# A gated mix of a spectral filter and a product-key lookup on one core: x tiles repeated by ScalarE, narrow inverse pieces joined, gates moved, another level of minima, a new order

## The chip, the cores and the metric

One NeuronCore of a Trainium2 chip runs the whole kernel in one launch. The metric is device time in microseconds, the median of several executions. Engines are named as the profile names them: PE (TensorE, matmuls), DVE (VectorE), ACT (ScalarE), POOL (GpSimd, here only the issuer of gathers) and SP (the issuer of plain loads and stores).

## The reference, cut to what matters

```
# x: (2048, 576); H = 32 heads, E = 64, dk = 128; u, v: (4096, 576)
g = sigmoid((x * gate_w).sum(-1, keepdims=True))
a = irfft2(rfft2(x) * (w_r + 1j * w_i))           # over the 2048 rows and the 576 columns
q = einsum("nd,dhc->nhc", x, w_q)                 # c = 2 * dk
s1, s2 = q[..., :dk] @ k1.T, q[..., dk:] @ k2.T   # (2048, 32, 64) each
i1, i2 = argmax(s1), argmax(s2)                   # top-1 of each; t1, t2 the scores there
e = i1 * 64 + i2                                  # one row of u and v for each token and head
p = softmax(one score)                            # 1, since one candidate is left
b = sum over h of  p * gelu(x . u[e]) * v[e]
out = g * a + (1 - g) * b
```

All of it is fp32. Each token needs 32 rows of u and v, gathered by an index that the scores give.

## The kernel before, in words

The 2048 tokens are 16 tiles of 128. The 32 heads are 8 chunks of 4. Tiles 0 to 9 are early (`E_T`), tiles 10 to 15 late (`L_SEQ`).

**Scores.** For each chunk `build_m` multiplies the keys into w_q (a high and a low part), and `scores` makes the scores of two tiles in a PSUM bank pair with 28 matmuls of 128x512. DVE takes the maxima (L385), ACT the signs of score minus maximum (L392), and then the position of the maximum is found in bf16: two halvings by `min` (L405, L413), a ramp added (L414), and a reduce over the 16 that are left (L416). The indices go to `ei` (early tiles) and `eil` (late ones).

**Early gathers.** `group(t, c)` issues four indirect DMAs on POOL (L465), one for each head of the chunk; each brings 128 rows of u and v (1152 numbers a partition) into a `uv` buffer. DVE multiplies with x and sums (the dot, L472, two instructions in the trace: the main one and the read of the accumulator), ACT applies gelu, and the v rows are added into `xn` in one of three ways, which the table `ROWS` picks: bit k set means that ACT scales the row (L493) and DVE adds it (L494), a clear bit a multiply-add on DVE (L498), and the value 16 sends the group through PE with a diagonal matrix (`dg`, L508).

**Late gathers.** For tiles 10 to 15 the 128 partitions are four heads by 32 tokens, so that one gather covers four heads. `quad(t, c)` issues four of them (L549), DVE makes the dots (L554) and PE sums over the heads with 16 narrow passes. For the dots each block of 32 tokens of x must stand on all four partition groups: `repeat(t)` does that on PE, with a matrix of identities (`rp`), for four blocks in two halves of the columns, and ACT drains each half out of PSUM (L541).

**Gates.** `gates(t, w)` is a DVE multiply with a sum over the columns, of x and the gate weights. The weights are spread over the partitions by `spread`: a load of one row, a matmul with a row of ones, a drain. This happens twice: for the early tiles near the start (L331), for the late ones in `close_gates` (L333), which then makes the sigmoid and its scalings `gsc` and `gone`.

**The transform.** `fold`, `f2`, `f4`, `f5` and `f6` are its steps in and back; `unit_back` does the first inverse step for a pair of frequencies: two pieces, each with eight passes of 256 columns into one bank (main) and four narrow passes into the other (the last 33 or 32 columns), drained by ACT (L806, L809). `invert` does the second inverse step; its result is scaled by `gsc` on ACT, and `mix` adds the lookup's part times `gone`.

**What sets the order.** Every operation is a job in a plan; the table `ORDER`, a list of job numbers, fixes in which order they are issued, and each engine runs its jobs in that order. Buffers come from rings: `uv` has 12 slots and gets more as other tiles die: the pairs that hold eight early x tiles (`pair0` to `pair3`), the area of the sign work and the room of the scores' operands. PSUM is four bank pairs (`bank`). Score pieces, repeats, transform pieces and sums share them.

Of the kernel before, what the change touches and what calls it, by code (L numbers as in the profile page):

```python
# [154 lines left out]
def tile_kernel(ctx, tc, xn, xT, x5, wqT, wq5, kT, wri, uv, gw, t_kr, t_fi, t_tw, t_io, out):  # L155
# [135 lines left out]
    lq = pp.tile([P, NL, H], F32, tag='lq', name='lq')  # L291
# [70 lines left out]
    def scores(c, tp):  # L362
# [53 lines left out]
        dv(0.06 + n * 256 / 960, lambda: nc.vector.tensor_reduce(im.ap[:, :2 * n].rearrange('p a h b -> p (a h b)'), q2()[:, :, :Q], AX.X, ALU.min), [im], keys)  # L416
# [110 lines left out]
    def repeat(t, after):  # L527
        x = xs[t]
        xr[t] = [buf(('xr', 'xn'), [P, D]) for _ in range(HPC)]
        for h in (0, 2):  # L530
            for r in range(2):
                ps = psum()
                cols = slice(r * 288, r * 288 + 288)

                def go(h=h, cols=cols, ps=ps):
                    for n in range(2):
                        lo = QB * (h + n)
                        mm(ps.ap[:, n, :288], rp.ap[lo:lo + QB, :], x.ap[lo:lo + QB, cols], start=True, stop=True)
                plan('PE', 0.7, go, [ps], [rp, x], after=after)
                for n in range(2):  # L540
                    ac(act(288), lambda n=n, h=h, cols=cols, ps=ps: actv(xr[t][h + n].ap[:, cols], ps.ap[:, n, :288], AF.Copy), [(xr[t][h + n], r)], [ps])  # L541
# [595 lines left out]
```

## Time and profile before

| what | us |
|---|---|
| median of three runs (lowest, highest) | 931.17 (930.18, 937.04) |
| the profiled execution | 935.08 |
| its span, first to last instruction | 933.3 |
| PE, DVE, ACT, POOL busy in the span | 870.9, 823.3, 594.9, 574.3 |
| share of the DMA queues: gathers, loads and stores | 84.9%, 11.6% |
| first gather issued | 34.41 |
| first quad's dot | 600.0 |

How to read it: a busy engine is one that has an instruction in flight, and durations of neighbours overlap, so a group's busy time can be less than its count times the mean of one; what an instruction costs a full engine is read from start to start. The shares are means over stages with different limits, so the prediction takes the busy times by stage, and the chain of waits (followed back from the last instruction) by stage. The DMA share is the time in which packets were under way, and GB/s what they moved. An fp32 matmul is two passes, two instructions in the trace.

### The profile page before, as it was taken

Reading aid. Unit: us, or ns where it says so; the run is one execution under the profiler, and the core shown is the slowest. Engines: PE = TensorE matmul, PEld = TensorE weight load, DVE = VectorE, ACT = ScalarE, POOL = GpSimd, SP = SyncE. Lnnn points to the kernel's source line nnn. Section 1 sums busy time; section 2 is a strip of 40 time slices with the busy share of each in tenths; the row PEclk is TensorE's granted clock in tenths of the full one; section 3 lists DMA queues with packets and bytes.
Section 4 is the critical chain, followed back from the end, with each engine's and each line's share of the span. In section 5 each row is a group of like instructions: output and inputs, shape, how many; then the busy total and the mean of one; then the engine's idle time right before and its main releaser. Section 6 shows DMA issues by size and latency. Waiting matters only on the chain.

```text
span 933.3 us, 16536 instructions
## 1 busy us (share of the span) xinstructions
PE 870.9 (93%) x5306; PEld 657.7 (70%) x5306; DVE 823.3 (88%) x1999; ACT 594.9 (64%) x2097; POOL 574.3 (62%) x516
## 2 busy tenths in 40 slices
PE   7999999999999999999999986788999989799986
PEld 6887888778877878787877775566565656466554
DVE  4899999999999999999999989999796867857577
ACT  5797988788868887979977869643333213232222
POOL 0366566765666766575667766677575666657561
PEclk9999999999999999999999998789999989999898
DMA  9999999999999999999999999999999998989997
GB/s 303 340 332 395 359 351 370 345 384 382 340 366 387 372 386 376 364 368 369 356 385 402 353 387 413 372 365 398 389 350 377 383 419 311 385 317 390 392 342 301
DMA packets 89467, 342.41 MB, mean 367 GB/s; under 512 B 9954, under 2 KB 10594, under 8 KB 89380
## 3 DMA queue, kind: packets, MB, share of 16 engines
q0 software_dynamic: 73728, 302.02, 84.9%
q1 hardware_dynamic: 15652, 39.33, 11.6%
q8 instruction: 42, 0.69, 0.3%
q14 instruction: 45, 0.37, 0.1%
HBM read 336.59 MB, written 4.72 MB: 366 GB/s over the span
## 4 chain that ended last, share of the span: by engine, by line
PE 49%; DVE 26%; ACT 8%; DMA 8%; issue 5%; another core or an unknown queue 2%; POOL 1%; DVEq 0%; SPq 0%; ACTq 0%
PE bank L256 49%; DVE uv L472 7%; DMA uv<-uv,ei 5%; DVE uv L554 4%; DVE xn L498 3%; DVE xn L494 3%; ACT area L392 3%; DVE area L385 2%; DMA pair<-uv,eiq 2%; DMA uv<-uv,eiq 1%; DVE pair L554 1%; ACT area L400 1%; DVE area L405 1%; DVE xn L522 1%
## 5 line engine op out<-in xcount | busy, mean ns | idle before, releaser
L465 POOL DMA_INDIRECT uv<-uv,ei x316 | 359.9, 1139 | 228.9 <-issue 61.8
L256 PE MATMUL bank<-mh,xt 128*128 128x512 f32 x768 | 261.6, 397 | 0.2 <-issue 0.2
L392 ACT ACTIVATE area<-bank,area 128x64 bf16<-128x64 f32 x1024 | 221.8, 352 | 20.8 <-DVE area L385 13.6
L549 POOL DMA_INDIRECT uv<-uv,eiq x141 | 155.0, 1099 | 88.8 <-PE bank L256 47.1
L472 DVE SCALAR_TENSOR_TENSOR uv<-uv,pair 128x576 f32<-128x576 f32 x253 | 184.9, 750 | 6.8 <-DMA uv<-uv,ei 5.5
L256 PE MATMUL bank<-ml,xt 128*128 128x512 f32 x448 | 174.8, 390 | 0.0
L256 PEld LDWEIGHTS bank<-mh,xt 128*128 128x128 f32 x768 | 144.2, 188 | 31.3 <-issue 0.7
L256 PE MATMUL bank<-uv,dg 128*32 128x288 f32 (+2 forms) x888 | 146.5, 416 | 13.7 <-ACT dg L508 5.5
L256 PE MATMUL bank<-mhx,xt 128*128 128x512 f32 x384 | 136.4, 402 | 0.2 <-DVE xn L522 0.2
L256 PEld LDWEIGHTS bank<-uv,dg 128*32 128x32 f32 (+2 forms) x888 | 82.6, 140 | 54.0 <-issue 9.7
L256 PE MATMUL bank<-fi,bt 128*128 128x289 f32 x384 | 106.1, 430 | 5.4 <-DVE area L750 2.4
L554 DVE SCALAR_TENSOR_TENSOR uv<-uv,xr 128x576 f32<-128x576 f32 x141 | 103.3, 752 | 6.5 <-DMA uv<-uv,eiq 2.9
L256 PEld LDWEIGHTS bank<-fi,bt 128*128 128x128 f32 x384 | 85.2, 247 | 27.3 <-issue 6.8
L498 DVE SCALAR_TENSOR_TENSOR xn<-uv,a,xn 128x576 f32<-128x576 f32 x125 | 101.2, 811 | 0.1
L256 PEld LDWEIGHTS bank<-ml,xt 128*128 128x128 f32 x448 | 84.2, 188 | 16.5
L493 ACT ACTIVATE uv<-uv,a 128x576 f32<-128x576 f32 x101 | 76.2, 777 | 13.9 <-DVE a L483 8.8
L256 PEld LDWEIGHTS bank<-mhx,xt 128*128 128x128 f32 x384 | 72.3, 188 | 17.9 <-ACT area L392 1.3
L385 DVE TENSOR_REDUCE area<-bank 128x16 f32<-128x1024 f32 x64 | 77.7, 1216 | 2.3 <-PE bank L256 2.1
L494 DVE TENSOR_TENSOR xn<-uv,xn 128x576 f32<-128x576 f32 x101 | 75.8, 751 | 0.2 <-ACT uv L493 0.2
L256 PE MATMUL bank<-mlx,xt 128*128 128x512 f32 x192 | 75.1, 391 | 0.0
L400 ACT ACTIVATE area<-area 128x256 bf16<-128x256 bf16 x192 | 72.2, 419 | 1.0
L555 ACT ACTIVATE b<-z 128x4 f32<-128x4 f32 x48 | 9.8, 204 | 82.3 <-DVE uv L554 52.1
(177 smaller groups left out, 1250.4 us busy)
## 6 DMA issues: line engine op xcount, KB each, us to landing
uv<-wqT SPq DMA_DIRECT2D x32, 512.0 KB
uv<-uv,ei POOLq DMA_INDIRECT x316
w<-wri SPq DMA_DIRECT2D x16, 289.0 KB
out<-xn SPq DMA_DIRECT2D x10, 288.0 KB
pair<-xn SPq DMA_DIRECT2D x8, 288.0 KB
uv<-uv,eiq POOLq DMA_INDIRECT x141
uv<-xT SPq DMA_DIRECT2D x8, 256.0 KB
uv<-wq SPq DMA_DIRECT2D x8, 256.0 KB
```

The lines of the kernel that those rows point to most:

```text
L256: after('PE', nc.tensor.matmul(*args, **kw))
L385: dv(dve(1024, True), lambda: nc.vector.tensor_reduce(mv.ap[:, 2 * tp:2 * tp + 2, :], ps.ap.rearrange('p a (g e) -> p a g e', e=E), AX.X, ...
L392: on('ACT', actv(sg.ap[:, j, g, :], ps.ap[:, j, g * E:g * E + E], AF.Sign, bias=mv.ap[:, 2 * tp + j, g:g + 1], scale=-1.0))
L400: ac(act(256), lambda b=b: actv(s2()[:, :, b * Q:b * Q + Q], s2()[:, :, b * Q:b * Q + Q], AF.Copy, bias=b / 4), [sg], [])
L465: on('POOL', nc.gpsimd.indirect_dma_start(out=g.ap.rearrange('p a d -> p (a d)'), out_offset=None, in_=uv, in_offset=bass.IndirectOffsetOn ...
L472: dv(0.68, lambda k=k, g=rows[k]: stt(g.ap[:, 0, :], g.ap[:, 0, :], 1.0, x.ap, op0=ALU.mult, op1=ALU.mult, accum_out=z.ap[:, k:k + 1]), [( ...
L493: ac(act_by(576), lambda v=v, s=s: actv(v(), v(), AF.Copy, scale=s()), [(rows[k], 1)], [a])
L494: dv(dve(576), lambda v=v: vt(y.ap, v(), y.ap, ALU.add), [y], [(rows[k], 1)])
L498: dv(0.73, lambda v=v, s=s: stt(y.ap, v(), s(), y.ap, op0=ALU.mult, op1=ALU.add), [y], [(rows[k], 1), a])
L549: on('POOL', nc.gpsimd.indirect_dma_start(out=g.ap.rearrange('p a d -> p (a d)'), out_offset=None, in_=uv, in_offset=bass.IndirectOffsetOn ...
L554: dv(0.68, lambda j=j: stt(rows[j].ap[:, 0, :], rows[j].ap[:, 0, :], 1.0, xr[t][j].ap, op0=ALU.mult, op1=ALU.mult, accum_out=z.ap[:, j:j + ...
L555: ac(0.1, lambda: actv(b.ap, z.ap, AF.Gelu_apprx_tanh), [b], [(z, j) for j in range(HPC)], table='gelu')
```

## The change

The line numbers of the order rows below are those of the changed program; L328 there is the gate, L529 and L530 the copies.

```diff
-    lq = pp.tile([P, NL, H], F32, tag='lq', name='lq')
+    lq = buf('lq', [P, NL, H])
...
-    def gates(t, w, junk=None):
+    def gates(t, w, to):
         x = xs[t]
...
+        dv(dve(576), lambda: stt(to.ap[:, :D], x.ap, 1.0, w.ap, op0=ALU.mult, op1=ALU.mult, accum_out=gz[:, t:t + 1]), [('gz', t), to], [x, w])
...
-        dv(0.06 + n * 256 / 960, lambda: nc.vector.tensor_reduce(im.ap[:, :2 * n].rearrange('p a h b -> p (a h b)'), q2()[:, :, :Q], AX.X, ALU.min), [im], keys)
+        dv(0.07 + n * 128 / 1920, lambda: vt(q2()[:, :, :Q // 2], q2()[:, :, :Q // 2], q2()[:, :, Q // 2:Q], ALU.min), keys, [])
+        dv(0.06 + n * 128 / 960, lambda: nc.vector.tensor_reduce(im.ap[:, :2 * n].rearrange('p a h b -> p (a h b)'), q2()[:, :, :Q // 2], AX.X, ALU.min), [im], keys)
...
     def repeat(t, after):
         x = xs[t]
         xr[t] = [buf(('xr', 'xn'), [P, D]) for _ in range(HPC)]
-        for h in (0, 2):
-            for r in range(2):
-                ps = psum()
...
+        for h in range(HPC):
+            part = lambda q, h=h: xr[t][h].ap[QB * q:QB * q + QB]
+            for q in range(2):
+                ac(act(576), lambda h=h, q=q, part=part: actv(part(q), x.ap[QB * h:QB * h + QB], AF.Copy), [(xr[t][h], q)], [x], after=after)
+            ac(act(576), lambda h=h: actv(xr[t][h].ap[2 * QB:], xr[t][h].ap[:2 * QB], AF.Copy), [(xr[t][h], 2)], [(xr[t][h], 0), (xr[t][h], 1)])
...
-    gw1 = buf('uv', ROW)
-    spread((gw1, 0), lambda: gw1.ap[:, 0, :])
...
-    for t in E_T:
-        gates(t, gw1)
...
-        for r, (z0, z1, use) in enumerate(((s, a, (mid, high)), (a, s, (low, mid)))):
-            lo, n = TAIL[r]
-            pt = f6(z0, z1, tw, use, [(lo, n, 256, use)])
...
+        zs, uses = ((s, a), (a, s)), ((mid, high), (low, mid))
+        pm, pt = psum(), psum()
...
+                for m in range(2):
+                    for k in range(2):
+                        mm(pm.ap[:, r, m * 256:m * 256 + 256], zs[r][k].ap[:, k, m * P:m * P + P], tw.ap[:, uses[r][k], :], start=k == 0, stop=k == 1)
...
+        def ends():
+            for k in range(2):
+                for r in range(2):
+                    mm(pt.ap[64 * r:64 * r + 33, 0, :256], zs[r][k].ap[:, k, 256:DF], tw.ap[:, uses[r][k], :], start=k == 0, stop=k == 1)
...
     def close_gates():
-        jg = psum()
         spread(gw2, lambda: gw2.ap)
+        for t in E_T:
+            gates(t, gw2, xs[t])
         for t in L_SEQ:
-            gates(t, gw2, jg)
+            gates(t, gw2, buf('f5', [P, ND * P]))
```

So a late tile's x is repeated by twelve ACT copies (each block of 32 tokens to two partition groups, and then the 64 partitions to the other 64) in place of eight matmuls and eight drains. The pair's wide passes of both pieces share one bank pair, and the narrow ones stand in one piece of their own. All 16 gates use one spread of the weights; an early gate writes its product over its own x tile, a late one into a buffer of `fold`. The reduce over 16 becomes a `min` of halves and a reduce over 8. `lq` moves to a pool that opens late. `ROWS` has 21 groups through PE (20 before), 81 rows scaled by ACT (102) and 145 multiply-adds (128). `ORDER` is another list throughout; three places show what that does.

DVE near the start: the gates of the first early tiles (`gz` is what they write, `pair` the x tiles, `area` the sign work) before,

```order
L320 TENSOR_TENSOR xt_1_28_373<-uv_297,xt_1_12_320 128x512
L331 SCALAR_TENSOR_TENSOR uv_128,gz<-pair_82,uv_128 128x576
L320 TENSOR_TENSOR xt_3_30_385<-uv_285,xt_3_14_327 128x512
L331 SCALAR_TENSOR_TENSOR uv_128,gz<-pair_82,uv_128 128x576
L320 TENSOR_TENSOR xt_1_32_399<-uv_303,xt_1_16_336 128x512
L385 TENSOR_REDUCE area<-bank_86 128x16
L405 TENSOR_TENSOR area<-area 128x512
L331 SCALAR_TENSOR_TENSOR uv_128,gz<-pair_83,uv_128 128x576
L413 TENSOR_TENSOR area<-area 128x16x16
```

and now, in the passage to the late part, between the last early dots (`z`), the folds (`f`) and the last indices:

```order
L328 SCALAR_TENSOR_TENSOR pair_85,gz<-pair_85,t_1151_6605 128x576
L494 SCALAR_TENSOR_TENSOR xn_1218<-uv_6767,a_6809,xn_1218 128x576
L328 SCALAR_TENSOR_TENSOR pair_84,gz<-pair_84,t_1151_6605 128x576
L468 SCALAR_TENSOR_TENSOR uv_6886,z_6861<-uv_6886,pair_85 128x576
L468 SCALAR_TENSOR_TENSOR uv_6851,z_6861<-uv_6851,pair_85 128x576
L670 TENSOR_TENSOR f_1171_6900<-pair_85 128x255
L414 SCALAR_TENSOR_TENSOR fe_6902<-im_6833 128x16
L468 SCALAR_TENSOR_TENSOR pair_82,z_6861<-pair_82,pair_85 128x576
```

The gates stood among the first scores and now stand where the early gathers end; the first dot of a quad follows soon behind them.

PE in the late part: before, a repeat (`xl`, `rp`) stands between transform pieces (`fi`, `bt`) and quads (`dg`, 32x288),

```order
L256 MATMUL bank_89<-pair_84,dg_7981 32x288
L256 MATMUL bank_89<-uv_7939,dg_7981 32x288
L256 MATMUL bank_87<-fi_6671,bt_6612 128x289 x6
L256 MATMUL bank_88<-xl_6771,rp_6211 128x288 x2
L256 MATMUL bank_86<-fi_6671,bt_6612 128x289 x6
L256 MATMUL bank_89<-pair_82,dg_8027 32x288
L256 MATMUL bank_89<-uv_7888,dg_8027 32x288
```

and now there is none; a pair's inverse (`tw`, `t`) has its narrow passes (33x256) in a piece by themselves, here ahead of the wide ones:

```order
L256 MATMUL bank_89<-tw_7578,t_1252_7804 33x256
L256 MATMUL bank_89<-tw_7578,t_1242_7695 33x256 x2
L256 MATMUL bank_89<-tw_7578,t_1252_7804 33x256
L256 MATMUL bank_86<-tw_7578,t_1242_7695 128x256
L256 MATMUL bank_86<-tw_7578,t_1252_7804 128x256
```

What stood on PE as a piece with its own bank pair, 24 times, is gone from this engine.

ACT in the late part: the copies of one tile (`xr`) now stand between the gelus (`b`), the twiddle tables (`tw`), and the drains of the inverse (`bt`) and of the forward step (`t`):

```order
L529 ACTIVATE xr_8005<-xl_6891 32x576
L544 ACTIVATE b_8022<-z_7926 128x4
L529 ACTIVATE xr_8005<-xl_6891 32x576
L711 ACTIVATE tw_7880<-bank_86 128x128
L709 ACTIVATE tw_7880<-bank_86 128x2x128
L529 ACTIVATE xr_8044<-xl_6891 32x576
L810 ACTIVATE bt_6559<-bank_89 32x2x128
L544 ACTIVATE b_8062<-z_8008 128x4
L810 ACTIVATE bt_6559<-bank_89 33x2x128
L807 ACTIVATE bt_6559<-bank_86 128x2x2x128 x2
```

The drains of repeats that stood here waited for PE; the copies wait for x alone.

More of the change, by code (lines that the diff above doesn't have):

```diff
@@ L446, in add_best @@
         mxv = lambda: mv.ap[:, t0:t1, :].rearrange('p t (h a) -> p t h a', a=2)
-        dv(0.1, lambda: vt(to(), mxv()[:, :, :, 0], mxv()[:, :, :, 1], ALU.add), [key], [(mv, tp) for tp in range(t0 // 2, t1 // 2)])
+        dv(0.1, lambda: vt(to(), mxv()[:, :, :, 0], mxv()[:, :, :, 1], ALU.add), [key], [(mv, tp) for tp in range(t0 // 2, (t1 + 1) // 2)])
     def soft(cand, to, n, kc, ks):
@@ L553, in quad @@
         for j in range(HPC):
-            dv(0.68, lambda j=j: stt(rows[j].ap[:, 0, :], rows[j].ap[:, 0, :], 1.0, xr[t][j].ap, op0=ALU.mult, op1=ALU.mult, accum_out=z.ap[:, j:j + 1]), [(z, j), (rows[j], 0)], [(xr[t][j], 0), (xr[t][j], 1)])
+            dv(0.68, lambda j=j: stt(rows[j].ap[:, 0, :], rows[j].ap[:, 0, :], 1.0, xr[t][j].ap, op0=ALU.mult, op1=ALU.mult, accum_out=z.ap[:, j:j + 1]), [(z, j), (rows[j], 0)], [(xr[t][j], r) for r in range(3)])
         ac(0.1, lambda: actv(b.ap, z.ap, AF.Gelu_apprx_tanh), [b], [(z, j) for j in range(HPC)], table='gelu')
@@ L652, in tile_kernel @@
         group(t, cc)
-    shuffle([lc], [lq], 0, NCH, [('lc', c) for c in range(NCH)], ['lq'])
-    soft(lambda: lq, lambda: lc, NL * H, 'lq', ['lc'] + [('lc', c) for c in range(NCH)])
-    for m, tag, pool, n in ((0, 'bt', 'la', 1), (0, 'f5', 'la', 2), (0, 'kr', 'la', 1), (0, 'krb', 'la', 1), (0, 'rp', 'la', 1), (0, 'eiq', 'la', 1), (1, 'xl', 'lb', NT - NE), (1, 'xr', 'lb', NXR), (1, 'fi', 'lb', 1), (1, 't2', 'lb', NT2), (1, 'tw', 'lb', 2), (1, 'tq', 'lb', 1), (1, 'w', 'lb', 2)):
+    shuffle([lc], [lq], 0, NCH, [('lc', c) for c in range(NCH)], [lq])
+    soft(lambda: lq.ap, lambda: lc, NL * H, lq, ['lc'] + [('lc', c) for c in range(NCH)])
+    for m, tag, pool, n in ((0, 'bt', 'la', 1), (0, 'f5', 'la', 2), (0, 'kr', 'la', 1), (0, 'krb', 'la', 1), (0, 'rp', 'la', 1), (0, 'eiq', 'la', 1), (0, 'lq', 'la', 1), (1, 'xl', 'lb', NT - NE), (1, 'xr', 'lb', NXR), (1, 'fi', 'lb', 1), (1, 't2', 'lb', NT2), (1, 'tw', 'lb', 2), (1, 'tq', 'lb', 1), (1, 'w', 'lb', 2)):
         home[tag] = pool
@@ L769, in tile_kernel @@
     TAIL = ((0, 33), (64, 32))
+    both_z = lambda s, a: [(x, k) for x in (s, a) for k in range(2)]
     front = []
@@ L907 @@
 TURN = ((0, 4), (4, 7), (7, 8))
-XL = (7, 7, 7, 7, 7, 7)
+XL = (7,) * 6
 XFI = 7
```

34 lines of the change are left out of this document (13 added, 21 removed), and 343 rows, old and new, of the table ORDER.

## The prediction

> **What bounds the kernel now.** First the page, for the engines' shares and the bytes.
>
> ```profile
> PE 870.9 (93%) x5306; PEld 657.7 (70%) x5306; DVE 823.3 (88%) x1999; ACT 594.9 (64%) x2097; POOL 574.3 (62%) x516
> DMA packets 89467, 342.41 MB, mean 367 GB/s; under 512 B 9954, under 2 KB 10594, under 8 KB 89380
> ```
>
> Three resources look nearly full over the whole span, and an average cannot say which one ends the waits. So next the busy time by stage: 75 to 550 us is scoring with early gathers, 550 to 625 us the passage to the late part, 625 to 925 us the transform with the late gathers (columns: PE, weight loads, DVE, ACT, POOL, clock, DMA share, GB/s).
>
> ```profile
> 75.00:550.00 475.00, 468.80 (x2843) 376.25 (x2842) 462.69 (x1063) 391.20 (x1462) 310.95 (x273) 1.00 0.98 371
> 550.00:625.00 75.00, 56.45 (x305) 43.63 (x304) 72.25 (x190) 54.54 (x208) 50.15 (x43) 0.82 1.00 382
> 625.00:925.00 300.00, 271.43 (x1541) 179.48 (x1539) 226.69 (x609) 88.19 (x233) 187.62 (x174) 0.95 0.96 371
> ```
>
> Scoring has PE and DVE both full. The passage has DVE full and PE not. In the late stage PE is busiest, DVE has a quarter free and ACT two thirds. Then the chain of waits, asked for 0 to 550 us and for 625 to 934 us:
>
> ```profile
> by line: PE bank L256 51.3%; DVE uv L472 10.7%; DMA uv<-uv,ei 5.3%; ACT area L392 4.8%; DVE xn L494 4.3%; DVE xn L498 4.2%; issue 4.1%; DVE area L385 3.0%; another core or an unknown queue 1.5%; ACT area L400 1.3%; DVE area L405 1.1%; DVE x
> by line: PE bank L256 53.6%; DVE uv L554 9.5%; issue 6.6%; DMA pair<-uv,eiq 4.9%; DMA uv<-uv,eiq 3.0%; DVE pair L554 2.5%; another core or an unknown queue 1.9%; DVE t L749 1.6%; DVE t L750 1.3%; POOL uv L549 1.1%; ACT xr L541 0.8%; ACT t L
> ```
>
> Half of each is PE. DVE has 23.3% of the first (10.7+4.3+4.2+3.0+1.1) and 14.9% of the second; the arrival of gathers 5.3% and 7.9%. I use these shares as weights: a microsecond of work removed from an engine gives back its share of the chain there. Last, whether the DMA could go faster than now:
>
> ```profile
> 745.00:750.00 5.00, 4.84 (x19) 4.17 (x20) 4.63 (x15) 1.13 (x4) 4.08 (x4) 1.00 1.04 423
> 770.00:775.00 5.00, 5.00 (x46) 2.57 (x44) 1.03 (x2) 3.94 (x6) 0.95 (x1) 1.00 0.33 135
> POOL uv L549 <- PE bank L256: 46.8, 24, 6.9
> ACT xr L541 <- PE bank L256: 24.6, 9, 5.5
> ```
>
> It moves 423 GB/s when gathers are queued. At 770 us PE was busy throughout and the DMA stood at a third: POOL waits 46.8 us in the late stage for PE to give back gather buffers. 300 us at 371 GB/s are 111.3 MB, 263 us at 423 GB/s, so the late stage could be up to 37 us shorter before the DMA alone held it.
>
> **The late PE work.** The 48 repeat matmuls go, each two passes in the trace; a piece of four passes and the next work start as follows. Beside them stand a pair's inverse piece (eight wide passes, four narrow), 16 passes of a quad, and a run of 24 full-width passes.
>
> ```profile
> L256 PE MATMUL bank<-xl,rp 32*128 32x288 f32 x96 | 18.7, 487 | 7.6 <-ACT xr L541 2.7 <-ACT tw L726 2.5 <-DVE xn L522 2.3
> 803.59 0.76 PE L256 MATMUL bank<-xl,rp 32*128 32x288 f32 x4
> 804.27 0.51 PE L256 MATMUL bank<-t,tw 128*128 128x289 f32 x1
> 786.34 2.87 PE L256 MATMUL bank<-tw,t 128*128 128x256 f32 x12
> 789.15 1.24 PE L256 MATMUL bank<-t,tw 128*128 128x289 f32 x4
> 881.16 1.18 PE L256 MATMUL bank<-uv,dg 128*32 128x288 f32 x16
> 882.27 6.12 PE L256 MATMUL bank<-fi,bt 128*128 128x289 f32 x24
> ```
>
> Start to start, a repeat piece takes 0.68 us; 24 of them are 16.3 us. The inverse piece takes 2.81 us for 12 passes, 0.234 each, so a pair's eight narrow passes cost 1.87 us. In the change they stand in one piece and alternate between the partitions from 0 and from 64. Whether two then run at once this trace does not show for them; the quads' passes, on four different partition groups, come at 0.074 us (1.18/16) where full-width ones take 0.255 (6.12/24). Bounds: nothing saved, or half. I take half, nearest to the quads: 0.94 x 7 pairs = 6.5 us, and keep 0. Together 22.8 us of PE work, times 53.6%: **-12.2 us** (-8.7 without the overlap). The 24 repeat pieces also give back their PSUM banks, a gain that I don't count. What is late next is the gather behind a freed buffer.
>
> **Early DVE.** Rows of 200 to 208 us give start-to-start times, and the groups the sizes of the minima:
>
> ```profile
> 201.39 0.74 DVE L472 SCALAR_TENSOR_TENSOR uv<-uv,pair 128x576 f32<-128x576 f32 x1
> ...
> 202.06 0.68 DVE L416 TENSOR_REDUCE im<-area 128x32 f32<-128x512 bf16 x1
> 202.66 0.74 DVE L494 TENSOR_TENSOR xn<-uv,xn 128x576 f32<-128x576 f32 x1
> 203.32 0.75 DVE L472 SCALAR_TENSOR_TENSOR uv<-uv,pair 128x576 f32<-128x576 f32 x1
> ...
> 207.31 0.81 DVE L498 SCALAR_TENSOR_TENSOR xn<-uv,a,xn 128x576 f32<-128x576 f32 x1
> 208.04 0.75 DVE L472 SCALAR_TENSOR_TENSOR uv<-uv,pair 128x576 f32<-128x576 f32 x1
> L416 DVE TENSOR_REDUCE im<-area 128x32 f32<-128x512 bf16 x30 | 20.4, 679 | 0.1
> L416 DVE TENSOR_REDUCE im<-area 128x16 f32<-128x256 bf16 x4 | 1.7, 417 | 0.1
> L413 DVE TENSOR_TENSOR area<-area 128x256 bf16<-128x256 bf16 x4 | 1.1, 274 | 0.0
> ```
>
> A dot takes 0.67, the reduce 0.60, an add 0.66, a multiply-add 0.73; each starts some 0.08 before the end of the last. Ten gates leave, dots in form: 10 x 0.67 = 6.7. Thirty reduces are halved, to 0.417-0.08 = 0.34, behind a new minimum of 0.274-0.08 = 0.19: 0.60 becomes 0.53, 2.0 saved; the four small ones come out even. The new ROWS has 17 more multiply-adds (+12.4), 21 fewer adds of rows that ACT scaled (-13.9) and one more add from PSUM (+0.7): -0.8. In all 9.5 us, times 23.3%: **-2.2** (0 to -9.5: DVE and PE are both full there, so one alone can give nothing). The first dot of a late quad stands behind about the same sum of DVE work in both orders, since the gates return just ahead of it. There they cost 6.7 x 14.9% = **+1.0**; were the passage, with DVE at 96%, the bound, 6.7. A gate now overwrites its x tile, so a pair of early tiles becomes a gather buffer only behind its two gates; POOL, which issues in order, waits for that. In the new order 48 gathers use these buffers (before: 44), so they come free no later; I cost it at nothing, as POOL has 112 of 300 us free, and at 0.67 for each of four pairs, 2.7, if it does not hide.
>
> **Early PE and ACT.**
>
> ```profile
> L256 PE MATMUL bank<-uv,dg 128*128 128x288 f32 x320 | 85.0, 411 | 6.7 <-ACT dg L508 5.5 <-ACT a L480 0.8 <-issue 0.2
> L256 PE MATMUL bank<-uv,dg 1*128 1x288 f32 x4 | 2.3, 723 | 0.0
> L493 ACT ACTIVATE uv<-uv,a 128x576 f32<-128x576 f32 x101 | 76.2, 777 | 13.9 <-DVE a L483 8.8 <-DVE area L405 1.9 <-issue 1.1
> L541 ACT ACTIVATE xr<-bank 128x288 f32<-128x288 f32 x48 | 17.7, 409 | 33.5 <-PE bank L256 27.4 <-DVE area L750 4.7 <-DVE uv L554 1.1
> L431 ACT ACTIVATE lq<-lc 32x48 f32<-32x48 f32 x16 | 4.6, 288 | 0.2
> L307 ACT ACTIVATE uv<-uv 128x512 f32<-128x512 f32 x8 | 5.1, 637 | 0.0
> ```
>
> A 21st group through PE adds 16 passes of 85.0/320 = 0.266: 4.2 us, at 51.3% **+2.2**. The early spread of the gate weights goes: 2.3 us, **-1.2**; its DMA is one row of 576 numbers on SP's queue, nothing. Twenty scalings leave ACT, 15.5 us, at its 6.1% (4.8+1.3) of the early chain **-0.9**.
>
> **The copies on ACT.** 48 drains (17.7 us) become 72 copies out of SBUF, 48 of 32 partitions and 24 of 64, all 576 wide. No such shape was run: below stands 288 ns (32x48), above 777 (128x576, scaled), nearest 637 (128x512). I take 0.70, in all 50.4 us, 32.7 more, and ACT goes from 88 to some 120 of 300 us: idle time covers it, if the order leaves the copies early enough. They wait for no PE, as the drains did (24.6 us), and their x lies loaded. Behind each stand gelus and PSUM drains that PE waits for. From the chain: 0.8% of 309 us is 2.5 us for 17.7 of drains; at that rate 32.7 would cost 4.6. Bounds 0 and 4.6; I take **+1.5**, as the wait for PE goes.
>
> **The sum.** -12.2-2.2+1.0+2.2-1.2-0.9+1.5 = -11.8 us: the span of 933.3 becomes 921.5. That execution took 935.08 and the median of the runs is 931.17, so the forecast for the median is 931.17-11.8 = **919.4 us**.
>
> **Rivals.**
> (a) Gathers pace it. The bytes stay, as the same 512 gathers go out. If the mean of 367 GB/s is what the memory gives over a span, what PE gains turns into waiting for data: **931**. For it: DMA shares of 0.96 to 1.00 in all three stages. Against it: 423 GB/s at 745 us, and 135 where POOL had no buffer. The Trainium skill ("DMA: Bandwidth & Descriptors", Specifications) derates DMA to 368 GB/s in the vendor's cost model: 342.41 MB by that are an estimate of 930 us. The mean agrees; the stretch at 423 does not.
> (b) ACT becomes the queue. **Slower**: if the copies stand in front of gelus and drains, so that their 50.4 us count at PE's share of 53.6%, that is +27.0 in place of +1.5: **945**. It turns into a loss from a quarter of the 50.4 us on the path. For it: ACT works in order and the new order threads copies between drains. Against it: ACT has 212 of 300 us free.
> (c) The clock takes it back.
>
> ```profile
> 865.00:870.00 5.00, 2.99 (x21) 1.34 (x13) 3.31 (x8) 1.72 (x5) 3.87 (x4) 1.00 1.01 413
> 870.00:875.00 5.00, 5.00 (x12) 2.76 (x13) 0.70 (x1) 1.92 (x6) 3.74 (x4) 0.51 1.03 423
> ```
>
> After PE was idle for 2 of 5 us it got a clock of 0.51. Less work may mean more such gaps: a late clock of 0.91 instead of 0.95 stretches the remaining 248.6 us by 10.9, at 53.6% +5.9: **925**. The Trainium skill ("TensorE: Matmul & The Clock Gate", Part 1) says that about 3.4 us of idling halves the clock; the rows agree with half.
> (d) All the late PE work lies on the path: 22.8 in place of 12.2, **909**; the 37 us of DMA room allow it. Against it: 46% of that chain is not PE.
>
> **How the numbers follow.** Forecast 0.48 (its own range 911 to 928), (a) 0.22, (b) 0.14, (c) 0.07, (d) 0.09. A measurement here tells about 1% from no change: 921.9 and 940.5. Faster: three fifths of the forecast, all of (d), little of (a) and (c): 0.29+0.09+0.06 = 0.44, and 0.02 for an order better than the shares say: 0.46. Slower: (b), 0.14. Same: 0.40. The range 906 to 938 leaves out most of (b) and the low end of (d). The widest doubt is the new order itself, whose rows carry no time.
>
> **What would show it.** Right: late PE busy near 250 us, POOL's late wait for PE well under 46.8, copies near 0.7 us, fewer stretches like 770 us, narrow passes in half the time. Wrong: ACT copies or drains at several per cent of the late chain (b); gather arrivals far above 7.9% of it (a); a late clock under 0.92 (c); scoring that ends later than before.

## The result and the profile after

| | before | after |
|---|---|---|
| median of the runs (lowest, highest), us | 930.67 (929.09, 937.04) | 953.74 (945.38, 957.95) |
| the profiled execution's span, us | 933.3 | 955.2 |
| ratio of the times, 95% interval | | 1.0263 [1.021, 1.0316] |

The change made the kernel 2.6% slower; the forecast was 1.3% faster, and 953.74 lies outside the range of 906 to 938. All ratios below leave out the runs of a kernel that took over 1.5% longer than its fastest in the same session, so where the runs spread widely a ratio is not the quotient of the two medians beside it. The page of after:

```profile
PE 852.5 (89%) x5222; PEld 654.7 (69%) x5222; DVE 821.2 (86%) x2028; ACT 618.7 (65%) x2107; POOL 573.3 (60%) x516
DMA packets 89464, 342.39 MB, mean 358 GB/s; under 512 B 9953, under 2 KB 10593, under 8 KB 89378
```

PE is busy for 18.4 us less than before, DVE for 2.1 less, ACT for 23.8 more, and the bytes are the same. So the work went where it was meant to go, and yet the span grew by 21.9 us. The busy time by stage of after (columns: PE, weight loads, DVE, ACT, POOL, clock, DMA share, GB/s):

```profile
75.00:550.00 475.00, 469.15 (x2871) 379.66 (x2870) 460.53 (x1085) 381.22 (x1454) 308.00 (x271) 1.00 0.98 370
550.00:625.00 75.00, 48.78 (x256) 38.34 (x254) 67.78 (x189) 56.53 (x197) 53.15 (x42) 0.82 0.97 369
625.00:925.00 300.00, 241.57 (x1401) 164.42 (x1400) 213.94 (x575) 113.66 (x242) 177.49 (x169) 0.92 0.90 348
```

Up to 550 us the two kernels are alike. In the passage PE is busy for 48.78 us in place of 56.45 and DVE for 67.78 in place of 72.25. From 625 to 925 us every engine but ACT is idler than before, the DMA share falls from 0.96 to 0.90 and the granted clock from 0.95 to 0.92. No engine is full there: they wait for each other. The chain of waits from 625 us to the end, and four of its longest pieces in order of time (start, us, what):

```profile
by line: PE bank L256 54.6%; DVE uv L543 7.9%; issue 7.3%; another core or an unknown queue 6.5%; DVE pair L543 2.8%; ACT bt L807 2.2%; ACT xr L529 1.4%; DVE xn L863 1.1%; DVE t L735 1.0%; DVE dg L547 0.9%; ACT xr L530 0.8%; ACT bt L810 0.7
...
746.93 9.61 another core or an unknown queue
760.09 7.40 PE bank L256 x24
...
780.00 6.43 another core or an unknown queue
...
810.21 7.76 issue
```

"another core or an unknown queue" went from 1.9% to 6.5% of this chain, "issue" from 6.6% to 7.3%. One core runs alone, so the first name can only mean that the profile found no releaser in time. Three pieces with no releaser, at 747, 780 and 810 us, take 23.8 us together, more than the span grew by. The first of them, as the timeline has it (start, us, engine, line, operation; in brackets the idle time before it and its releaser):

```profile
746.01 2.22 PE L256 MATMUL bank<-area,tw 128*128 128x289 f32 x8
...
746.18 0.75 DVE L787 TENSOR_TENSOR t<-t,t 128x578 f32<-128x578 f32 x1
...
748.06 2.11 PE L256 MATMUL bank<-t,tw 128*128 128x289 f32 x8
...
754.80 0.94 POOL L538 DMA_INDIRECT uv<-uv,eiq  x1 [0.30 <-issue]
756.56 0.76 DVE L735 TENSOR_TENSOR area<-bank,w 128x578 f32<-128x578 f32 x1 [9.63 <-remote]
...
758.70 0.21 ACT L544 ACTIVATE b<-z 128x4 f32<-128x4 f32 x1 [11.93 <-DVE pair L543]
...
760.09 7.39 PE L256 MATMUL bank<-tw,t 128*128 128x256 f32 x24 [9.91 <-ACT tw L709]
...
768.84 1.53 POOL L538 DMA_INDIRECT uv<-uv,eiq  x1 [13.10 <-PE bank L256]
```

The two groups of matmuls (`f4`) that DVE's L735 and its neighbours wait for have their modelled ends at 748.23 and 750.17. L735 starts at 756.56, 0.03 us after PE's semaphore is raised, which the trace has at 756.53: 8.3 us after the first of these ends, 6.4 after the second. In a trace that comes later in this text (e16) the same instruction starts right behind the first of the two groups. So DVE waited for a completion that was reported at least 6, and likely 8 us after the matmuls should have ended. Behind it everything stops: ACT waits 11.93 us for DVE, PE 9.91 for ACT, and POOL 13.10 for buffers that PE has not given back.

In stretches of 2 us of the same place:

```profile
748.00:750.00 2.00, 2.00 (x9) 1.34 (x8) 0.00 (x0) 0.00 (x0) 1.39 (x3) 1.00 0.92 329
750.00:752.00 2.00, 0.17 (x1) 0.00 (x0) 0.00 (x0) 0.00 (x0) 1.69 (x2) 1.00 0.98 394
752.00:754.00 2.00, 0.00 (x0) 0.00 (x0) 0.00 (x0) 0.00 (x0) 1.39 (x3) 1.00 1.03 422
754.00:756.00 2.00, 0.00 (x0) 0.00 (x0) 0.00 (x0) 0.00 (x0) 1.44 (x2) 0.75 1.02 422
756.00:758.00 2.00, 0.00 (x0) 0.00 (x0) 1.44 (x4) 0.00 (x0) 0.00 (x0) 0.50 1.03 424
```

PE, DVE and ACT are all idle from 750.2 us on, and only gathers move. The clock halves at 755, after the stall has begun: here it follows, and does not cause.

I call such a completion a **late end** and measure it by the time from the last modelled end of a matmul that raises PE's semaphore to the next raise in the trace. That is a lower bound, since an earlier matmul may be meant. A little over half are under 0.12 us. After 550 us, before has 41 of them above 1 us and 9 above 2 us; after has 50 and 23, the longest 7.8 us. All the lags together are 110 us in before, 166 in after. In the whole run of after, DVE's updates are late 2 times in 988 and ACT's 2 times in 620: of what the trace has, it is TensorE's alone.

### The profile page after: what moved, and what is told of

Read it like the earlier page. It is cut to its first block, busy times and chain, and to the rows that moved or that the text cites. A ratio compares the mean times of both kernels' runs of the same rounds, so it can differ in the third digit from the quotient of the medians.

```text
span 955.2 us, 16353 instructions
## 1 busy us (share of the span) xinstructions
PE 852.5 (89%) x5222; PEld 654.7 (69%) x5222; DVE 821.2 (86%) x2028; ACT 618.7 (65%) x2107; POOL 573.3 (60%) x516
## 5 line engine op out<-in xcount | busy, mean ns | idle before, releaser
L461 POOL DMA_INDIRECT uv<-uv,ei x319 | 367.6, 1152 | 227.7 <-issue 62.3
L256 PE MATMUL bank<-mh,xt 128*128 128x512 f32 x768 | 265.5, 401 | 0.0
L538 POOL DMA_INDIRECT uv<-uv,eiq x135 | 141.9, 1051 | 106.7 <-PE bank L256 64.5
L256 PE MATMUL bank<-uv,dg 128*32 128x288 f32 (+1 forms) x876 | 147.5, 415 | 10.4 <-ACT dg L504 4.7
L256 PEld LDWEIGHTS bank<-uv,dg 128*32 128x32 f32 (+1 forms) x876 | 84.3, 142 | 50.8 <-issue 10.3
L494 DVE SCALAR_TENSOR_TENSOR xn<-uv,a,xn 128x576 f32<-128x576 f32 x144 | 117.0, 815 | 0.2 <-ACT xn L492 0.2
L543 DVE SCALAR_TENSOR_TENSOR uv<-uv,xr 128x576 f32<-128x576 f32 x135 | 99.4, 754 | 14.8 <-ACT xr L530 5.4
L489 ACT ACTIVATE uv<-uv,a 128x576 f32<-128x576 f32 x81 | 62.0, 790 | 11.0 <-DVE a L479 5.3
L538 POOL DMA_INDIRECT pair<-uv,eiq x47 | 51.6, 1098 | 25.3 <-issue 8.2
L256 PE MATMUL bank<-tw,t 128*128 128x256 f32 (+3 forms) x176 | 44.2, 433 | 24.3 <-ACT tw L709 10.1
```

The costliest lines, as they stand in the source:

```text
L256: after('PE', nc.tensor.matmul(*args, **kw))
L461: on('POOL', nc.gpsimd.indirect_dma_start(out=g.ap.rearrange('p a d -> p (a d)'), out_offset=None, in_=uv, in_offset=bass.IndirectOffsetOn ...
L489: ac(act_by(576), lambda v=v, s=s: actv(v(), v(), AF.Copy, scale=s()), [(rows[k], 1)], [a])
L494: dv(0.73, lambda v=v, s=s: stt(y.ap, v(), s(), y.ap, op0=ALU.mult, op1=ALU.add), [y], [(rows[k], 1), a])
L538: on('POOL', nc.gpsimd.indirect_dma_start(out=g.ap.rearrange('p a d -> p (a d)'), out_offset=None, in_=uv, in_offset=bass.IndirectOffsetOn ...
L543: dv(0.68, lambda j=j: stt(rows[j].ap[:, 0, :], rows[j].ap[:, 0, :], 1.0, xr[t][j].ap, op0=ALU.mult, op1=ALU.mult, accum_out=z.ap[:, j:j + ...
```

## The experiments

The kernels ran in six sessions, each with its own runs of before, and all ratios are against those. One difference between them only came out as they were compared: in some, TensorE's ends come late, in before too; in the others they never do, but for two at the program's very end.

| session | chip number on record | late ends | before, us | profiled runs: late ends above 1 us / above 2 us |
|---|---|---|---|---|
| 1 (the result) | none | yes | 930.67 | before 41/9, after 50/23 |
| 2 (e1 to e4) | 7 | no | 903.66 | 2/2 in each |
| 3 (e5 to e8) | 1 | yes | 926.5 | e5 41/9, e6 34/10, e7 48/23, e8 35/8 |
| 4 (e9 to e12) | 10 | no | 904.87 | 2/2 in each |
| 5 (e13 to e15) | 13 | yes | 932.15 | e13 57/29, e14 47/20, e15 35/14 |
| 6 (e16 to e18) | 1 | no | 903.38 | 2/2 in each |

The expectations below speak of chips of a slow and a fast kind. Number 1 stands at session 3, with late ends, and at session 6, without: if it names the same chip, the chip alone does not decide. The count of late ends is not the time either: e8 and e15 are both the kernel before with 35 of them, and took 913.75 and 924.79 us.

The letters are those of the expectations: A, the new order costs and the edits give; B, the copies on ACT; C, the joined piece holds PSUM banks; D, the late gates keep gather buffers; E, the late ends.

### The edits in the old order, and two of them alone

e1 takes all edits, with `ROWS` and `ORDER` of before (a job that is new stands where its counterpart stood):

```diff
-ROWS = {0: (0, 16, 16, 9, 0, 6, 2, 0), 1: (8, 4, 0, 1, 9, 16, 2, 16),
+ROWS = {0: (0, 16, 16, 3, 5, 2, 2, 10), 1: (0, 3, 1, 5, 4, 16, 3, 16),
...
```

> All five edits of the change, but each instruction stands where its counterpart stood in the old order: a copy where the drain of its repeated rows stood, the joined passes where the two separate ones stood, the gates of the early tiles spread between the old late spread and the sigmoid. Theory A (the new order costs the time, the edits give what was forecast): 915 to 927 us. Theory B (72 copies on ScalarE hold up the drains behind them, rival b): 940 to 955. Theory C (the joined narrow passes hold two PSUM banks of four and starve TensorE): 940 to 955.

Measured: 931.88, **1.0315 [1.0286, 1.0344]**. The expected times of e1 to e4 are those of a session where before takes 931 us; here it took 903.66, so the ratios are compared. A's 927 would be 0.996: A falls, as the edits cost 3.15% in the old order. The new order was made for them. The ranges of B and C end at 955, a ratio of 1.026: the cost is above them too.

e2 is before with the copies alone:

```diff
-                        mm(ps.ap[:, n, :288], rp.ap[lo:lo + QB, :], x.ap[lo:lo + QB, cols], start=True, stop=True)
...
+            for q in range(2):
+                ac(act(576), lambda h=h, q=q, part=part: actv(part(q), x.ap[QB * h:QB * h + QB], AF.Copy), [(xr[t][h], q)], [x], after=after)
+            ac(act(576), lambda h=h: actv(xr[t][h].ap[2 * QB:], xr[t][h].ap[:2 * QB], AF.Copy), [(xr[t][h], 2)], [(xr[t][h], 0), (xr[t][h], 1)])
```

> The kernel before, with the repeated x rows made by ScalarE copies and nothing else changed. A: 919 to 931 us, as the 16 us of TensorE passes go. B: 940 to 950. C: 919 to 931.

Measured: 906.87, **1.0041 [1.0025, 1.0057]**. The 24 repeat pieces go from PE, and the time rises by 0.4%. No range held it: A's ends at 1.000 and B's begins at 1.010. The cost of rival (b), 1.5%, falls, but the gain is gone too. Where: in the waits of 550 to 650 us, e2 has, and then e3, whose repeats stay on PE (columns: us, times, longest),

```profile
PEld bank L256 <- ACT f L675: 19.2, 5, 11.7
PE bank L256 <- ACT f L675: 16.8, 4, 11.2
```

```profile
PEld bank L256 <- ACT f L682: 8.5, 4, 4.7
PE bank L256 <- ACT f L682: 6.2, 3, 4.5
```

PE waits up to 11.7 us for the ACT step of a fold (`f`): copies stand in front of it in ACT's order. With the old order that happens in e1 and e9 too (20.8 and 18.2 us); in the new order the same wait is 7.4.

e3 is before with the joined narrow passes alone:

```diff
-            pt = f6(z0, z1, tw, use, [(lo, n, 256, use)])
+        pm, pt = psum(), psum()
...
+                for r in range(2):
+                    mm(pt.ap[64 * r:64 * r + 33, 0, :256], zs[r][k].ap[:, k, 256:DF], tw.ap[:, uses[r][k], :], start=k == 0, stop=k == 1)
```

> The kernel before, with the narrow inverse passes of a pair joined and nothing else changed. A: 925 to 931 us. B: the same. C: 940 to 950.

Measured: 909.73, **1.0067 [1.0047, 1.0088]**. In the old order the joined piece costs 0.7%, between the ranges of A (up to 1.000) and C (from 1.010).

e4 is after, new order and all, with the narrow passes apart again (the same edit backwards).

> The changed kernel in its new order, with the narrow passes of a pair apart again. A: 950 to 962 us, no gain or a little slower than the changed kernel. B: 948 to 958. C: 930 to 940.

Measured: 917.26, **1.0151 [1.0129, 1.0173]**. Beside e16 below (0.9943, the changed kernel itself in a session of the same kind) that is 2.1% slower, although no range of the expectation held 1.0151: in the new order, which was made for it, the joined piece pays. C, a cost that it would have in any order, falls.

### The gates, the minima, and the pair of kernels again

e5 is before with all gates late, e6 before with the extra level of minima:

```diff
-    for t in E_T:
-        gates(t, gw1)
...
+        for t in E_T:
+            gates(t, gw2, xs[t])
```

```diff
+        dv(0.07 + n * 128 / 1920, lambda: vt(q2()[:, :, :Q // 2], q2()[:, :, :Q // 2], q2()[:, :, Q // 2:Q], ALU.min), keys, [])
```

> The kernel before, with the gates of all 16 tiles in the late part (those of the early tiles as in the run with the old order: one after every 24 positions from the late spread on) and nothing else changed. Theory D (gathers pace the kernel, and a gate that reads a pair tile late keeps four of the 18 gather buffers from the gathers for some 40 us, so that the DMA engines run empty between 550 and 625 us): 1.015 to 1.025 of the time before, DMA share of 550 to 625 us under 0.92. Theory F (10 more DVE instructions of 0.68 us in the late part, 6.7 us, and no more): 1.001 to 1.008.

> The kernel before, with the one more level of minima and nothing else changed. D: 0.999 to 1.002 of the time before, since DVE's early time is not what gathers wait for. My prediction's term of 2.2 us: 0.996 to 0.999.

Measured: e5 936.79, **1.0181 [1.0054, 1.0307]**; e6 926.62, 1.0103 [0.9957, 1.0248]. The runs of before in session 3 spread from 911 to 930, so e6 says only that no large effect is there. e5 costs 1.8%; in the passage, beside e8 (before, in the same session),

```profile
550.00:625.00 75.00, 52.91 (x259) 40.96 (x261) 66.77 (x174) 53.11 (x203) 43.96 (x39) 0.76 0.93 342
```

```profile
550.00:625.00 75.00, 55.64 (x300) 43.56 (x299) 70.94 (x190) 51.13 (x191) 49.42 (x42) 0.82 0.99 376
```

POOL issued 39 gathers instead of 42 and the DMA fell from 376 to 342 GB/s. It fits D: tiles that wait for their gates become gather buffers later. It is not more than a fit: the DMA share is 0.93 where D said under 0.92, and the interval reaches down to 1.0054, which F would allow.

e7 is after, e8 before, unchanged, one more time.

> The changed kernel, on the chip of these runs. Theory E (what the changed kernel lost beyond its edits came from late ends of matmuls, which the runs of the four first experiments don't show): 1.010 to 1.018 of the time before. D alone (its own places of the gates and gathers cost it): 1.022 to 1.032 on every chip.

> The kernel before, for its profile on the chip of these runs. E: a span near 903 us and hardly a matmul whose end is signalled over 0.2 us after the modelled one after 550 us. Otherwise: a span near 931 us with 41 of them over 1 us, as in the first profile.

Measured: e7 936.47, **1.0186 [1.0035, 1.0338]**, just above E's range, with an interval that holds E's range and D's; e8, one execution, 913.75, with 35 late ends above 1 us: neither the 903 without them nor the 931. Here I first saw that the loss moves with the session, and that session 3 had late ends where session 2 had none.

### Gates in both orders, half the bytes, zero weights

e9 is the old order with copies, joined passes and minima, and the gates left early; e10 is after with the ten early gates put back to the start:

```diff
+    gw1 = buf('uv', ROW)
+    spread((gw1, 0), lambda: gw1.ap[:, 0, :])
...
+    for t in E_T:
+        gates_early(t, gw1)
...
-        for t in E_T:
-            gates(t, gw2, xs[t])
```

> The kernel before in its old order with three of the edits, the copies, the joined passes and the level of minima; the gates of the early tiles stay early. Theory D (the DMA engines pace the kernel; late gates keep gather buffers and make them run empty): 1.002 to 1.012 of the time before, near the sum of the two runs with one edit each (1.004 and 1.007), with the DMA engines empty for 10 to 15 us up to the last gather. Theory G (the edits together are too much for ScalarE or the PSUM banks, gates or not): 1.025 to 1.035, as with all five edits in the old order.

> The changed kernel in its new order, with the gates of the early tiles early again (at the places of the kernel before, from a gather buffer as there). If the late gates are the loss in the new order too: 0.998 to 1.010 of the time before. If the rest of the new order is: 1.015 to 1.026.

Measured: e9 921.49, **1.0182 [1.0141, 1.0222]**, which neither range held; e10 906.1, 1.0022 [0.9998, 1.0046]. From e1 to e9 the early gates give back 1.3%; from after (0.9943 in e16) to e10 they cost 0.8%. So late gates cost in the old order and gain in the new one. e10 fell into the range for a loss by late gates, but in a session in which after itself loses nothing, so it does not speak for that loss.

e11 is before with late gathers of half the bytes. It fetches other rows than the reference needs, and uses the same half for dots and sums:

```diff
-                on('POOL', nc.gpsimd.indirect_dma_start(out=g.ap.rearrange('p a d -> p (a d)'), out_offset=None, in_=uv, in_offset=bass.IndirectOffsetOnAxis(ap=eiq.ap[:, t - NE, c * HPC + j:c * HPC + j + 1], axis=0)))
+                on('POOL', nc.gpsimd.indirect_dma_start(out=g.ap[:, 0, :], out_offset=None, in_=uv.rearrange('n (a d) -> (n a) d', a=2), in_offset=bass.IndirectOffsetOnAxis(ap=eiq.ap[:, t - NE, c * HPC + j:c * HPC + j + 1], axis=0)))
...
-                    mm(pd.ap[QB * j:QB * j + QB, r, :288], dg.ap[:, j, :], rows[j].ap[:, 1, r * 288:r * 288 + 288], start=c == 0, stop=c == NCH - 1)
+                    mm(pd.ap[QB * j:QB * j + QB, r, :288], dg.ap[:, j, :], rows[j].ap[:, 0, r * 288:r * 288 + 288], start=c == 0, stop=c == NCH - 1)
```

> The kernel before, with the late gathers bringing rows of half the length (576 numbers in place of 1152, so wrong rows, and the late sums are made from the same half); all instructions of the engines stay. Theory D: 192 late gathers times 0.295 MB less, 57 MB or some 135 us of DMA time; the engines' own work then sets the pace, so 0.88 to 0.95 of the time before. Theory P (TensorE's chain paces the late part, as the chain of waits says and my forecast took it): 0.985 to 1.005.

Measured: 898.81, **0.9937 [0.9919, 0.9955]**: 56.6 MB less bring 0.6%. P's range held it, D's did not. Its late part in two halves:

```profile
625.00:760.00 135.00, 132.15 (x801) 92.22 (x800) 118.66 (x308) 49.27 (x123) 96.12 (x91) 1.00 0.76 223
760.00:885.00 125.00, 119.30 (x720) 76.38 (x719) 99.98 (x280) 37.73 (x105) 90.19 (x82) 1.00 0.76 226
```

With a quarter of the DMA free, PE is busy for 251.5 of 260 us and carries 66.9% of that late chain. Where ends are not late, the late part of before has two resources close together: gathers, and right behind them PE.

e12 is after with zeros in the table from which the weights of the late sums are made. So the late tiles' lookup part is left out of the output, and each instruction stays:

```diff
-    rp = np.tile(np.eye(QB), (P // QB, P // QB))
+    rp = np.zeros((P, P))
```

> The changed kernel with the 32-column table of ones set to zero, so that the late sums' matmuls multiply by zero (their part is left out of the result); every instruction stays. If the late ends of matmuls behind those sums come from what the matmuls compute (a limit on TensorE's current): none over 2 us after 550 us but the last, and 0.97 to 0.99 of the changed kernel's time. If they come from how the instructions stand: the three long ones, 4 to 8 us, at the same instructions, and the changed kernel's time (1.012 to 1.026 of before).

Measured: 897.27, **0.9919 [0.9898, 0.994]**. The changed kernel's instructions are faster than before in session 4. The trace has none of the three stalls. Whether the zeros took them away or the session never had them, e12 alone could not say.

### The session or the data

Hence all three side by side, in what was a session with late ends: e13 (after), e14 (e12's kernel) and e15 (before).

> The changed kernel once more. Theory E (it is slower only through matmuls that end late): on a chip where the kernel before takes 901 to 908 us, 0.985 to 1.000 of it; on one where it takes 911 to 937, 1.015 to 1.030 with three ends over 4 us late. Theory O (the new order and the edits cost it everywhere): 1.015 to 1.030 on both.

> The changed kernel with the late sums' matmuls multiplying by zero (their part is left out of the result). On a chip without late ends, if zeros save no time: within 0.3 per cent of the changed kernel in the same call. On a chip with late ends: none over 2 us but the last and 1 to 3 per cent less than the changed kernel if what is multiplied brings them; within 0.5 per cent of it, with the same three, if not.

> The kernel before, for its profile on this chip: about 41 matmul ends over 1 us late after 550 us on a chip of the slow kind, 2 on one of the fast kind.

Measured: e13 951.78, **1.0154 [1.0063, 1.0245]**; e14 955.6 (four runs, 939.08 to 957.25, before's median 932.15); e15, one execution, 924.79. On e13 both theories said the same, and it lies in their range; e14 is within 0.5% of e13, and e15 has 35 late ends above 1 us where about 41 were expected. The zero weights have the same stalls; the first, in e14:

```profile
748.27 2.11 PE L256 MATMUL bank<-t,tw 128*128 128x289 f32 x8
...
755.38 0.76 DVE L735 TENSOR_TENSOR area<-bank,w 128x578 f32<-128x578 f32 x1 [7.43 <-remote]
```

The same kernel took 897.27 in session 4 and 955.6 here. So zeros in these sums do not take the late ends away, and the late ends come and go with the session. The other matmuls kept their data.

And once more the changed kernel, in what became a session without them, with e17, in which the late sums use the whole width of the array (8 matmuls of 128 columns of weights by 72 columns in place of 8 of 32 by 288, so the sums are not those of the reference), and e18, e10's kernel again:

```diff
-                    mm(pd.ap[QB * j:QB * j + QB, r, :288], dg.ap[:, j, :], rows[j].ap[:, 1, r * 288:r * 288 + 288], start=c == 0, stop=c == NCH - 1)
+                    mm(pd.ap[:, r, 72 * j:72 * j + 72], dg.ap.rearrange('p j e -> p (j e)'), rows[j].ap[:, 1, r * 288 + 72 * j:r * 288 + 72 * j + 72], start=c == 0 and j == 0, stop=c == NCH - 1 and j == HPC - 1, skip_group_check=True)
```

> The changed kernel once more. Theory E: on a chip of the fast kind (before 901 to 908 us) 0.985 to 1.000 of before; on the slow kind 1.015 to 1.030. Theory O: 1.015 to 1.030 on both.

> The changed kernel with each late sum made of eight matmuls over all 128 columns, 72 of the row's columns each, in place of eight over 32 columns, 288 each, four at once (so the late sums' values are wrong; instructions and streamed columns in sum stay). On the slow kind of chip, if the groups of columns bring the late ends: hardly one over 2 us, and 0.97 to 0.99 of the changed kernel in this call. If the rate of instructions does: the three long ones at the same places, within 0.7 per cent of the changed kernel. On the fast kind: within 0.5 per cent of it, since TensorE's time is nearly the same.

> The changed kernel in its new order with the gates of the early tiles early, as before. On the slow kind of chip, if the late gates are the loss there: 0.998 to 1.008 of the kernel before. If the late ends behind the late sums are, whatever the gates: 1.012 to 1.028. On the fast kind: 1.000 to 1.005, as measured before.

Measured: e16 899.13, **0.9943 [0.9923, 0.9962]**; e17 917.06, 1.0139 [1.0103, 1.0176]; e18 905.83, 1.0025 [1.0007, 1.0043]. The changed kernel, not one letter different, is 0.6% faster than before here: E's range held it, O's did not. The place of the first stall, in e16:

```profile
730.03 2.22 PE L256 MATMUL bank<-area,tw 128*128 128x289 f32 x8
...
730.18 0.76 DVE L787 TENSOR_TENSOR t<-t,t 128x578 f32<-128x578 f32 x1
...
732.08 2.11 PE L256 MATMUL bank<-t,tw 128*128 128x289 f32 x8
732.28 0.76 DVE L735 TENSOR_TENSOR area<-bank,w 128x578 f32<-128x578 f32 x1 [1.35 <-PE bank L256]
...
734.43 0.21 ACT L544 ACTIVATE b<-z 128x4 f32<-128x4 f32 x1 [4.43 <-DVE pair L543]
```

The same instructions at the same distances, up to DVE's L735: it starts 2.25 us after the first `f4` matmul here, 10.55 us after it in after. The wait has a releaser by name again. The late part of e16 by time, its chain from 625 us on, and two of its waits over the whole run:

```profile
625.00:895.00 270.00, 245.64 (x1512) 168.04 (x1512) 231.05 (x619) 118.23 (x251) 183.46 (x170) 0.99 1.01 407
```

```profile
by line: PE bank L256 45.9%; DMA uv<-uv,eiq 10.1%; DVE uv L543 6.8%; DMA pair<-uv,eiq 6.4%; issue 4.2%; DVE pair L543 3.7%; DMA uv<-uv,ei 3.0%; ACT bt L807 2.3%; DVE xn L863 1.6%; ACT xr L529 1.2%; DVE xn L490 1.0%; DVE t L735 1.0%; POOL uv
```

```profile
PEld bank L256 <- issue: 27.7, 68, 2.4
POOL uv L538 <- PE bank L256: 24.6, 33, 3.6
```

"another core or an unknown queue" does not appear in this chain, the clock is 0.99, and gathers now carry 19.5% of it (10.1+6.4+3.0). e17 was expected within 0.5% of e16 and is 2.0% slower: with its wide sums PE is busy for 865.0 us in place of 836.1. As it met no late ends, it says nothing on whether the narrow column groups bring them.

Together: in sessions with late ends the change costs 2.6%, 1.9% and 1.5%; in the one without, it gives 0.6%. From the one to the other kind, before loses 27.3 us (903.38 to 930.67) and after 54.6 (899.13 to 953.74): the difference of 27.3, less the 4.3 that the change gains, is the 23.1 of the result.

Where after loses its time can be read by laying its trace beside e16's, as both run the same instructions in the same order. DVE's instructions start 4.3 us later in after at 550 us and 6.1 at 625. By L787 of the first place the lag is 16.0 us (746.18 against 730.18), and at L735 just behind it 24.3 (756.56 against 732.28). At the second place it goes from 26.8 to 33.0 (L735 at 786.45), at the third from 34.8 to 44.1 (L700 at 824.81), and the spans end 54.9 apart. The three places make 23.8 us of that; the rest comes in smaller steps, most of them behind 625 us. No version that I ran beats both kernels where ends come late.

## Why the prediction was wrong, step by step

**The failed step** is the cover given to the late PE work: "What is late next is the gather behind a freed buffer". What was late next were PE's own completions. A term for them is missing from the sum: between sessions 6 and 1 it is +27.3 us more for after than for before. The rows of before held the hint: 1.9% of the late chain at "another core or an unknown queue" in a program on one core, and "issue" at 6.6%. I read past both, though "issue" is a weak hint (4.2% in e16, which has no late ends). "The widest doubt is the new order itself, whose rows carry no time" was the right doubt, and I gave it no price. In after the three long ones stand directly behind a late sum, at `f4` or `f6` pieces, for which DVE or ACT waits next, then PE and POOL. That the place in the order makes them long is what the repeated traces suggest: the same three places have late ends of 5 us and more in after, e7, e13 and e14, and in before, e8 and e15 none is above 4 us but that at the program's end (4.8). No run changed such a place alone, so why these places are hit stays open.

**Late PE work, -12.2.** The weight of 53.6% came from an execution with late ends. A kernel with the repeats still on PE in a session without them is e3; its chain from 625 us on:

```profile
by line: PE bank L256 37.4%; DMA uv<-uv,eiq 12.4%; DVE uv L554 11.7%; DMA pair<-uv,eiq 9.0%; issue 4.6%; DVE pair L554 3.5%; DVE t L749 1.2%; DVE dg L558 1.1%; DVE t L785 1.0%; DVE area L554 1.0%; POOL uv L549 0.9%; DVE t L862 0.9%; DVE t L
```

By 37.4% the 22.8 us would be an estimate of 8.5. And e8, before itself in session 3, has PE at 68.0% of its late chain: the share is not a property of the kernel, and as a weight it was soft. The instructions behaved as priced. PE is 18.4 us less busy, where -22.8 with the 21st group and the spread made -20.9. A joined narrow piece:

```profile
780.08 1.06 PE L256 MATMUL bank<-tw,t 128*33 128x256 f32 x8
```

That is 0.13 us a pass in place of 0.234 (the mean of wide and narrow passes in a piece of before), nearly the half that I took. What it is worth is another matter: without late ends the whole change gives 4.3 us instead of 11.8. e3, e11 and e16 show a part of the reason. The late part of e16 runs its DMA at a share of 1.01, and gather arrivals are 19.5% of its late chain. That is not PE's relief: e3 has them at 21.4% (12.4+9.0), and the 7.9% that the prediction read belong to a session with late ends. So "What is late next is the gather behind a freed buffer" describes the sessions without late ends, and there it leaves a gain of 4.3 us.

**Early DVE, gates, minima.** DVE's total fell by 2.1 us, where 2.0 + 0.8 were expected, since the gates stay on DVE. "I cost it at nothing" for the gate on pair tiles: in the old order it cost 1.8% together with the rest of the edit (e5), in the new order the late gates give 0.8% (e16 beside e18). The minima: no effect that could be seen (e6).

**Early PE and ACT, +2.2, -1.2, -0.9.** No run took these apart. PE and DVE are as busy at 75 to 550 us as before.

**Copies on ACT, +1.5.** The price of one was right; in after,

```profile
L529 ACT ACTIVATE xr<-xl x48: 664/682/687, 561.3 to 897.0; 32x576 f32<-32x576 f32 x48
L530 ACT ACTIVATE xr<-xr x24: 664/682/685, 592.1 to 899.6; 64x576 f32<-64x576 f32 x24
```

0.68 us for both shapes, against 0.70. But the place was wrong: with the old order they hurt in the passage, ahead of the folds, and not ahead of gelus in the late part, and the copies alone cost 0.4% net (e2), although PE loses 24 pieces. In the new order that wait is no longer than in e3 (7.4 and 8.5 us).

**Rivals.** (a) With 367 GB/s as what the memory gives, it fell: e16 moves the same bytes at a mean of 380, and 407 in the late part, and e3, with the repeats on PE, at 377. In a weaker form, gathers as the next limit in the late part, it may be why e16 gains so little. The Trainium skill ("DMA: Bandwidth & Descriptors", Specifications) has 368 GB/s as a derate; 380 over a whole span is above it, and the measurement decides. (b) The change is slower, as (b) said, but for another reason; copies alone cost 0.4%. (c) The late clock fell to 0.92, where its sign was a clock under that, and to 0.50 behind the first stall; but the clock halves some 5 us into an idle time that began without it. The Trainium skill ("TensorE: Matmul & The Clock Gate", Part 1) says that an idle window of about 3.4 us brings the half rate, and that the windows run freely, whatever the program does. 755.0 less 750.2 is 4.8 us, in which one whole window finds room: the trace agrees. (d) No.

**The signs that I named.** POOL's late wait for PE, "well under 46.8", was 55.4 from 625 to 925 us in after and 23.1 in e16: it pointed at the stall in the one and at the relief in the other. Gather arrivals "far above 7.9%" came in e16, and in e3 as well. Edits do not add up: +0.4% (e2) and +0.7% (e3) alone, +1.8% with the minima (e9), +3.15% with the gates (e1), and -0.6% in the order and with the `ROWS` made for them (e16).

## What to carry to other kernels

Before weighting work by a chain of waits, find out what its pieces without a releaser are; on one core, "another core or an unknown queue" can mean a completion that came later than the profile thinks. And read the shares in more than one execution: PE's late share was 53.6% in one trace of before and 68.0% in another. A change that comes with a new order is neither its edits nor its order: the same edits were 3.15% slower in one and 0.6% faster in the other, so try an edit in an order that was made for it. And compare two kernels in more than one session before believing 2%.

## What the runs showed of the hardware

- TensorE's completions can be reported up to 7.9 us late, in some sessions and not in others, for the same program, and with zeros as the weights of the late sums too (late in e14, on time in e12). A late sum raises PE's semaphore four times, once for each group of 32 columns. In e16 the four raises ahead of the place above stand at 730.10, 730.14, 730.18 and 730.22, and those of the two `f4` groups at 732.26 and 734.21, each 0.01 to 0.12 us behind its modelled end. In after the same six stand at 749.42, 750.12, 750.86, 752.25, 756.53 and 758.00, where the ends are modelled at 746.06 to 746.08, 748.23 and 750.17: the raises of the sum are late first, some 0.7 us or twice that apart, and `f4`'s come behind them. In such sessions raises are also missing from the trace (after 550 us 273 in after for 299 matmuls that make one; in e16 298 for 296), so this pairing, in order, is the likely one and not certain. They are missing for DVE as well, which hardly has a late one: 988 raises in after for 1372 instructions that make one, 1374 in e16.
- The Trainium skill ("TensorE: Matmul & The Clock Gate", Part 3, on the per-tile semaphore tail) says that raises by the matmuls of several tiles go one behind the other, 26 ns each, and that a raise by the last tile alone is enough. The 0.04 us of e16 are near that; the 0.7 to 1.4 us of after are not. A kernel with one raise for each late sum was not run, and e17 met a session without late ends: whether either would be free of them, what in a session brings them, and whether the matmuls or only their reports are late, stays open.
- Between sessions 6 and 1, before loses 3.0% (903.38 to 930.67 us) and after 6.1% (899.13 to 953.74).
- ACT copies 32 or 64 partitions of 576 columns in 0.68 us, to other partitions than it reads.
- Two narrow fp32 passes that write to partitions from 0 and from 64 run nearly two at once: 0.13 us each, where the pieces of before, wide and narrow passes together, take 0.234.
